# A written table for the order of TensorE's tasks and of the loads, in a kernel of windowed attention and a multiplicative feed-forward layer

## The chip, the core and the metric

The kernel runs on one core of a Trainium2 chip. The metric is the device time of one execution in microseconds, the median of several runs; the times and places in the text are microseconds, places from the start of the profiled span.

## The reference

Attention over 4 batches, 8 heads, 768 positions and head dimension 64, in which each query sees the first 4 keys (sinks) and the last 128; then a feed-forward layer that is linear but for one product.

```python
scores = scale * np.matmul(q, k.transpose(0, 1, 3, 2))
keep = is_sink | in_window              # first 4 keys, or 0 <= i - j < 128
a = softmax(np.where(keep, scores, -1e9))
x = (a @ v).transpose(0, 2, 1, 3).reshape(3072, 512)
out = ((x @ w1) * (x @ w2)) @ w3 @ w_out      # w1, w2: 512x1024; w3: 1024x1024; w_out: 1024x512
```

All inputs and the output are float32 in memory.

## The kernel before, in words

Everything is computed in bf16 with float32 sums. The loads turn float32 into bf16 on the way (they are issued by GpSimd, L108 to L141), but for the first block of w3, which SyncE loads as it is (L162). The two last matrices are folded into one on the chip, w3 @ w_out (`w3o`). TensorE's work is cut into tasks, each a generator that a planner steps through (L468 to L690); the first step is the part on TensorE, the next ones are copies and products on ScalarE and VectorE, and a last one may be a DMA on SyncE. The names of the tasks, which the text uses, are a kind and its indices:

- `t3.i.j` (`fold_w3`): eight 128x128 transposes of block i of w3 (four each for the float32 block 0: t3.0.0 and t3.0.4), and a copy out of PSUM. `fm.i.n` (`fold_mm`, L380): the fold of block i with half n of w_out: eight matmuls of 256 columns.
- `tpk.b.t`, `tpq.b.t`: transposes of k and q of batch b, 256 positions t (t is 0, 1 or 2), for batches 0 and 1; batch 0 holds positions in pairs and is transposed in pieces of 64 rows (`transposes_paired`, L228). Batches 2 and 3 are transposed by DMAs that SyncE issues (`td`, L237).
- `sc.b.r.t` (`scores`): the scores of a pair of heads r, with exponentials on ScalarE (L284) and the mask on VectorE (L288); some carry the scores of the sinks (L270). `sv.b`: the sinks' values. `av.b.r.t` (`values`): weights times values, then divided by their sum on VectorE (L314, L317).
- `xt.b.r.t`: transposes of x for batches 0 and 1 (`x_transposes`), and `xd` (L337), the same by DMA on SyncE for batches 2 and 3.
- `g.b.c.dt.h` (`gate`, L350): one of 8 column blocks dt of x @ w1 (h is 0) or x @ w2 (h is 1), four matmuls of 256 or 384 columns; h = 0 is copied by ScalarE, h = 1 multiplied by VectorE. `p.b.m` (`project`, L390): 128 rows of the output, eight matmuls of 512 columns, a copy by ScalarE and a DMA.

Four PSUM buffers (`mm`) are shared by all tasks but the scores, which have two of their own (`sc`). A task on TensorE needs its buffer free, so it waits for the copy of the fourth task back.

The planner has made-up arrival times of the loads (`arrive`, L407 to L466) and costs of each step. As it runs while the program is built, the order that comes out is fixed in the program: `pe_pick` (L586) takes at each point the task that can start first by its model, then by priority; ScalarE, VectorE and SyncE take the step that is ready first. If the model sees TensorE idle over 0.5 us before 40 us, and a PSUM buffer free, it puts in matmuls of zeros (`keep_busy`, L404; `pz` in the profile).

The order of the loads is a list (L146). After three of them come the mask tables that GpSimd makes (`affine_select`: identities, masks, sink masks); the framework may still move instructions on GpSimd, and does: it puts q and v of batch 2 ahead of most of its k. Each load is a DMA of 0.25 MB, as bf16; a half of w_out has 0.5 MB, and 0.125 MB the blocks of v and those of batches 1 to 3. In the trace GpSimd stops when eight are on their way (at 17.8 it goes on as the first half of w_out lands). k and q of batch b lie in the buffers of batch b - 2.

## Time and profile before

| | us |
|---|---|
| median of 4 runs (lowest, highest) | 202.45 (202.33, 202.77) |
| the profiled execution | 202.95 |
| its span in the profile | 201.2 |
| TensorE busy | 194.8 |
| VectorE busy | 114.5 |
| ScalarE busy | 102.6 |
| zero matmuls, recorded | 39 |

In the profile PE is TensorE's matmuls, PEld its weight loads, DVE VectorE, ACT ScalarE, POOL GpSimd and SP SyncE. A group of instructions is given by its line, engine, operation, what it writes and reads, its shape and number; then its busy time, the mean of one in ns, and the idle time before it with what ended that. A line of waits reads: who, for whom, us in total, times, longest. The chain of work that ended last follows the program back from its last instruction; a piece of it has its start, its length and what ran. The recorded length of one matmul (309 ns for a gate's) holds its latency, as they overlap; the pace is read from the chain, where eight fold matmuls take 0.87.

### The profile page before, as it was taken

What the parts mean: (1) busy time and instruction counts of PE and PEld (TensorE: products, weight loads), DVE (VectorE), ACT (ScalarE), POOL (GpSimd) and SP (SyncE); (2) the same over time, 40 slices, a digit from 0 to 9 for tenths busy, and PEclk for the clock granted to TensorE, in tenths of its full rate; (3) what the DMA queues carried; (4) which work ended last, traced back from release to release, by engine and by line L of the source; (5) the groups of instructions that cost most, each with busy time, mean ns of one, the idle gap of its engine ahead of it and who ended that gap; (6) DMA issues with size and microseconds to landing.
All of it is one profiled execution on the core that took longest, in us unless ns stands there. A gap on an engine that the chain in (4) does not pass through costs nothing.

```text
span 201.2 us, 4659 instructions
## 1 busy us (share of the span) xinstructions
PE 194.8 (97%) x1875; PEld 126.5 (63%) x1888; DVE 114.5 (57%) x267; ACT 102.6 (51%) x175; POOL 72.9 (36%) x98
## 2 busy tenths in 40 slices
PE   7999999999999999999999999999999999999992
PEld 2556987887887786566666555565666556665440
DVE  5176636695788767169777656473788404444000
ACT  2106424734866775676757466455756343333331
POOL 7991566769996998351341000000000000000000
PEclk9999999999999999999999999999999999999999
DMA  6999999999999999999999999612004251000242
GB/s 135 166 161 197 187 192 199 193 170 155 154 153 164 151 156 150 133 185 185 155 130 133 155 158 316 134 54 57 0 0 54 88 173 57 0 0 0 107 155 105
DMA packets 99158, 26.27 MB, mean 131 GB/s; under 512 B 88896, under 2 KB 95040, under 8 KB 99136
## 3 DMA queue, kind: packets, MB, share of 16 engines
q0 software_dynamic: 75952, 14.42, 90.5%
q1 hardware_dynamic: 23184, 11.54, 29.2%
q8 instruction: 15, 0.25, 0.5%
q14 instruction: 7, 0.06, 0.1%
HBM read 29.36 MB, written 6.29 MB: 177 GB/s over the span
## 4 chain that ended last, share of the span: by engine, by line
PE 96%; DVE 1%; issue 1%; ACT 0%; ACTq 0%
PE pg L350 42%; PE po L390 20%; PE av L310 7%; PE pw L380 7%; PE sc L276 6%; PE pz L404 5%; PE tp L369 2%; PE tp L228 2%; PE xt L326 1%; PE tp L214 1%; PE sp L270 1%; PE vp L251 1%; DVE qT L231 1%; DVE kT L231 1%; ACT o_sb L394 0%
## 5 line engine op out<-in xcount | busy, mean ns | idle before, releaser
L350 PE MATMUL pg<-xT,w_sb 128*128 128x384 bf16 (+1 forms) x576 | 90.1, 309 | 0.0
L350 PEld LDWEIGHTS <-w_sb 128*128 128x128 bf16 x576 | 53.7, 98 | 25.8 <-issue 1.7
L354 DVE TENSOR_TENSOR ab<-a_sb,pg 128x384 bf16<-128x384 f32 (+1 forms) x72 | 36.5, 508 | 32.1 <-PE pg L350 26.7
L284 ACT ACTIVATE ex<-sc 128x1024 bf16<-128x1024 f32 (+1 forms) x48 | 44.9, 955 | 12.9 <-PE sc L276 12.1
L357 ACT COPY a_sb<-pg 128x384 f32<-128x384 f32 (+1 forms) x72 | 31.9, 443 | 36.5 <-DVE ab L354 19.8
L390 PE MATMUL po<-w3o,ab 128*128 128x512 bf16 x180 | 43.0, 379 | 0.6
L288 DVE TENSOR_TENSOR am<-ex,maskt 128x1024 bf16<-128x1024 bf16 (+1 forms) x48 | 30.3, 641 | 6.2 <-ACT ex L284 6.2
L390 PEld LDWEIGHTS <-ab 128*128 128x128 bf16 x192 | 18.2, 98 | 20.1 <-issue 0.3
L394 ACT COPY o_sb<-po 128x512 f32<-128x512 f32 x24 | 14.0, 585 | 26.4 <-PE po L390 26.1
L317 DVE TENSOR_TENSOR xn<-av,rec 128x256 bf16<-128x256 f32 x48 | 20.4, 425 | 1.7
L111 POOL DMA_DIRECT2D vN<-in_v_dram x18 | 16.1, 903 | 10.1 <-DMA kN<-in_k_dram 5.9
L310 PE MATMUL av<-vN,am 128*128 128x65 bf16 x352 | 18.9, 193 | 0.0
L310 PEld LDWEIGHTS <-am 128*128 128x128 bf16 x352 | 16.9, 97 | 3.1 <-DVE am L288 0.2
L111 POOL DMA_DIRECT2D kN<-in_k_dram x18 | 16.1, 901 | 7.2 <-DMA kN<-in_k_dram 4.0
L111 POOL DMA_DIRECT2D qN<-in_q_dram x18 | 16.1, 895 | 6.3 <-DMA vN<-in_v_dram 3.1
L314 DVE RECIPROCAL rec<-av 128x4 f32<-128x4 f32 x48 | 8.6, 178 | 14.5 <-PE av L310 14.3
L380 PE MATMUL pw<-wo_sb,w3t 128*128 128x256 bf16 x128 | 15.8, 273 | 0.0
L276 PE MATMUL sc<-qT,kT 64*128 64x128 bf16 (+1 forms) x256 | 13.9, 238 | 0.4 <-DVE kT L231 0.4
L404 PE MATMUL pz<-ksbd 128*128 128x512 bf16 x39 | 12.4, 468 | 1.3 <-DVE ksbd L164 1.3
L380 PEld LDWEIGHTS <-w3t 128*128 128x128 bf16 x128 | 11.9, 98 | 1.5 <-issue 0.2
L310 PE MATMUL av<-vs,es 128*128 128x130 bf16 x64 | 12.3, 221 | 0.0
L276 PEld LDWEIGHTS <-kT 64*128 64x128 bf16 x256 | 8.2, 94 | 6.1 <-issue 4.4
(62 smaller groups left out, 115.1 us busy)
## 6 DMA issues: line engine op xcount, KB each, us to landing
out_dram<-o_sb SPq DMA_DIRECT2D x24, 256.0 KB, 2.3
vN<-in_v_dram POOLq DMA_DIRECT2D x24, 128.0 KB, 8.3
kN<-in_k_dram POOLq DMA_DIRECT2D x18, 128.0 KB, 7.6
qN<-in_q_dram POOLq DMA_DIRECT2D x18, 128.0 KB, 7.8
w_sb<-in_moe_w_dram POOLq DMA_DIRECT2D x8, 256.0 KB, 10.2
ab<-in_moe_w_dram POOLq DMA_DIRECT2D x7, 256.0 KB, 9.4
wo_sb<-in_moe_w_out_dram POOLq DMA_DIRECT2D x2, 512.0 KB, 9.6
qN<-in_q_dram POOLq DMA_DIRECT2D x3, 256.0 KB, 9.4
```

Of the source, the lines that this page charges most:

```text
L111: nc.gpsimd.dma_start(out=dst, in_=rows(src, b, kb))
L276: nc.tensor.matmul(sc[:, e, c:c + n], kT[b][hp, r, kb * P:(kb + 1) * P], qT[b][hp, r, qb * P:qb * P + n], start=True, stop=True)
L284: nc.scalar.activation(ex[:, :, c0:], sc[:, :, c0:], ACTF.Exp, scale=scale)
L288: nc.vector.tensor_mul(am[:, :, c0:], ex[:, :, c0:], mk)
L310: nc.tensor.matmul(o, lhs, rhs, start=(n == 0), stop=(n == len(todo) - 1), skip_group_check=True)
L317: nc.vector.tensor_mul(xns[b, t][:, :, r, :, :], av[:, :, :, 0:D], rec[:].to_broadcast([P, 2, 2, D]))
L350: nc.tensor.matmul(pg[:], w_sb[:, kk, dt * P:(dt + 1) * P], xT[b][:, kk, tk], start=(kk == 0), stop=(kk == NP - 1))
L354: nc.vector.tensor_mul(ab[b][:, dt, tk], gate_a.pop((b, c, dt))[:], pg[:])
L357: nc.scalar.copy(a_sb[:], pg[:])
L380: nc.tensor.matmul(po[:], w3T[i][:, j, :], wo_sb[:, j, n0:n1], start=(j == 0), stop=(j == KFF - 1))
L390: nc.tensor.matmul(po[:], ab[b][:, kk, m * P:(m + 1) * P], w3o[:, kk, :], start=(kk == 0), stop=(kk == KFF - 1))
L404: nc.tensor.matmul(pz[:], idle[:, 0:P], idle[:, 0:512], start=True, stop=True)
```

## The change

It has these parts.

- The planner's choice on TensorE is replaced by a table of names, `PLAN`, in which every task of TensorE stands once; `pe_pick` takes the next name and waits for it. On the other engines the planner goes on as before, with new costs. A change of tiling of TensorE's array (full, rows for scores, columns for the paired transposes) costs 0.096 in its model.
- The loads come in another order: k and q of positions 0 to 511 of batch 0 first, one half of w_out a load later than before, its second half two later, w1 and w2 behind all of w3. GpSimd is told to keep the order as written. The identities are made after the second load, the masks after the third, the sink masks after the fourth.
- Zero matmuls are counted with 0.43 us each up to 6.5 us and 0.22 after, less one, and only if three PSUM buffers are free. In the built program there are 13 instead of 40.
- The paired transposes of batch 0 are cut into halves (two pairs of heads), and their copies, those of x and those of the output go to ScalarE or VectorE, as the planner finds, instead of to a fixed one.
- In the planner's order of SyncE, a DMA transpose of batch 2 or 3 now comes at least 12 us after TensorE's transposes of batch 0 or 1 that read the same buffer (`late`).

The diff, cut:

```diff
-    order = [("q", 0, 0), ("w3", 6), ("w3", 3), ("k", 0, 0), ("v", 0, 0), ("wo", 0, 256), ("wo", 256, 512),
-             ("w1", 0, 256), ("w3", 4), ("w3", 1), ("w3", 2), ("v", 0, 1), ("k", 0, 1), ("q", 0, 1),
...
+    order = [("q", 0, 0), ("k", 0, 0), ("k", 0, 1), ("q", 0, 1), ("v", 0, 0), ("w3", 4), ("wo", 0, 256), ("w3",
+             3), ("wo", 256, 512), ("w3", 2), ("w3", 7), ("v", 0, 1), ("w3", 5), ("w3", 6), ("w3",
+             1), ("w1", 256, 512), ("w2", 256, 512), ("k", 0, 2), ("q", 0, 2), ("w1", 768, 1024),
+             ("w2", 768, 1024), ("w2", 512, 768), ("v", 0, 2), ("w2", 0, 256), ("w1", 0, 256),
+             ("w1", 512, 768)] + [
              ("qkv", b, 0, 6) for b in range(1, B)]
-    EARLY = 3
...
+    masks = {2: make_idents, 3: make_masks, 4: make_sink_masks}
+    with tc.manual_schedule(engines={mybir.EngineType.Pool}):
+        for n, x in enumerate(order):
+            if n in masks:
+                masks[n]()
+            load(*x)
...
-    def transposes_paired(src, dst, t):
+    def transposes_paired(src, dst, t, r0, me):
...
-        tp = ps_mm.tile([P, NP, 2, P], BF16, tag="mm", name="tp")
-        for r in range(NP):
+        tp = ps_mm.tile([P, 2, 2, P], BF16, tag="mm", name="tp")
+        for r in range(2):
...
-        nc.scalar.copy(xT[b][:, r0:r0 + 2, t * 256:(t + 1) * 256],
-                       xt[:].rearrange("p r i m -> p r (i m)"))
+        copy_on(me, xT[b][:, r0:r0 + 2, t * 256:(t + 1) * 256], xt[:].rearrange("p r i m -> p r (i m)"))
...
-        nc.scalar.copy(o_sb[:], po[:])
+        copy_on(("p", b, m), o_sb[:], po[:])
...
+    PLAN = """
+        t3.0.4 tpq.0.0.2 tpq.0.0.0 tpk.0.0.0 tpk.0.0.2 sc.0.0.0 t3.0.0 sc.0.1.0 tpk.0.1.0 tpq.0.1.2
+        tpq.0.1.0 tpk.0.1.2 sc.0.2.0 sv.0 av.0.0.0 av.0.1.0 sc.0.3.0 t3.4.0 sc.0.0.1 sc.0.1.1 av.0.2.0
+        xt.0.0.0 fm.4.0 av.0.3.0 t3.3.0 fm.0.0 xt.0.2.0 sc.0.2.1 sc.0.3.1 fm.3.0 fm.3.1 fm.0.1 t3.2.0
+        fm.4.1 t3.7.0 fm.2.1 fm.2.0 fm.7.1 av.0.0.1 t3.5.0 av.0.1.1 fm.7.0 av.0.2.1 fm.5.1 av.0.3.1
+        xt.0.0.1 t3.1.0 fm.5.0 t3.6.0 xt.0.2.1 fm.1.0 fm.1.1 g.0.0.2.0 g.0.1.3.0 g.0.1.3.1 tpq.0.2.0
...
+    SWITCH = 0.096
...
+        est = max([free["pe"] + (SWITCH if tiled(k) != tiling else 0.0)] + [arrive[x] + HOP for x in k["loads"]])
...
+    plan = [tuple(int(x) if x.isdigit() else x for x in name.split(".")) for name in PLAN.split()]
+
     def pe_pick():
+        if plan:
+            k = tasks[plan[0]]
+            est = earliest(k)
+            return None if est is None else (0, k, est)
         best = None
...
-                if gap > 0.5 and start < WARM_UNTIL and rings["mm"][0][0] is not None \
-                        and rings["mm"][0][0] <= max(free["pe"], START):
-                    keep_busy(int((gap - 0.25) / 0.22))
+                spins = int((max(0.0, min(start, 6.5) - max(free["pe"], START)) / 0.43
+                             + max(0.0, start - max(free["pe"], START, 6.5)) / 0.22) - 1.0)
+                if spins > 0 and gap > 0.5 and start < WARM_UNTIL and all(
+                        c[0] is not None and c[0] <= max(free["pe"], START) for c in rings["mm"][:3]):
+                    keep_busy(spins)
```

## The prediction

> **What bounds the kernel now.** I read the page first: who is busy, the chain that ended last, and what zero matmuls (`pz`, L404) cost.

> ```profile
> PE 194.8 (97%) x1875; PEld 126.5 (63%) x1888; DVE 114.5 (57%) x267; ACT 102.6 (51%) x175; POOL 72.9 (36%) x98
> ...
> PE pg L350 42%; PE po L390 20%; PE av L310 7%; PE pw L380 7%; PE sc L276 6%; PE pz L404 5%; PE tp L369 2%; PE tp L228 2%; PE xt L326 1%; PE tp L214 1%; PE sp L270 1%; PE vp L251 1%; DVE qT L231 1%; DVE kT L231 1%; ACT o_sb L394 0%
> ...
> L404 PE MATMUL pz<-ksbd 128*128 128x512 bf16 x39 | 12.4, 468 | 1.3 <-DVE ksbd L164 1.3
> ```

> TensorE is the bound almost from end to end, and 5% of the chain is multiplication by zero. The waits of TensorE say the same:

> ```profile
> PE pz L404 <- DVE ksbd L164: 1.3, 1, 1.3
> PE sc L276 <- DVE kT L231: 0.4, 1, 0.4
> PE sp L270 <- DVE qT L231: 0.3, 1, 0.3
> ```

> So the other engines matter only where they would make TensorE wait, and the time can fall in two ways: fewer zero matmuls, or fewer tiling changes. Then the chain in order of time (start, us, what):

> ```profile
> 1.33 6.90 PE pz L404 x18
> 8.23 0.87 PE tp L369 x8
> 9.10 1.29 PE pz L404 x6
> 10.40 0.57 PE tp L228 x16
> ...
> 13.26 0.59 PE tp L228 x16
> 13.87 1.24 DVE kT L231
> 15.15 0.50 PE sc L276 x8
> 15.65 0.32 PE vp L251
> 15.98 1.29 PE pz L404 x6
> 17.27 0.44 PE sc L276 x8
> ...
> 88.34 0.55 PE sc L276 x12
> 88.88 0.76 PE pg L350 x4
> ...
> 96.47 0.65 PE pg L350 x4
> ```

> The zeros at the start last until 8.23, though asked one issue at a time the trace has the raw w3 block landed at 4.20 and q at 6.85 (its transposes start at 10.40). The granted clock in the trace is full only from 7.12 on: till then zeros are 0.43 apart, later 0.215. From 18 on there are no zeros, and TensorE is full. Last pair above: a gate of four matmuls takes 0.65, and 0.76 right behind scores.

> **The change, part by part.**

> *Zeros.* The order of the built kernels has 40 before (39 recorded) and 13 after (6, then half of t3.0, then 7). On the chain the old ones take 5.3% of 201.2 = 10.7. New: 6 x 0.43 = 2.6, from 1.33 to 3.9; t3.0.4 waits for the block (4.20) and for the fp32 identity, which is behind q and k at GpSimd (about 4.0); its 4 transposes take 0.44 warm, so about 0.87 cold, to 5.1; the 7 zeros run at 0.43 up to 7.12 and then at 0.215, to about 7.6. That is 5.1 of zeros: 5.6 less. This is a gain only where real work fills the place, so I place the work.

> *First attention.* q (6.85) is transposed at 7.6 instead of 10.4. k is now second at GpSimd: 1.3 behind q (two 0.25 MB loads behind q land 1.33 and 1.29 apart), 8.2. Copies are halved (about 0.69 on VectorE, 0.6 on ScalarE, from the 128x512 rows of L207 and L330, instead of 1.23 for one at L231) and lie on both engines. VectorE has the four copies of ones_s ahead of them, and these wait for the sink masks, now behind two more loads at GpSimd: about 8.1, so VectorE's first copy ends near 9.3. The first scores start about 9.4 instead of 15.15. Behind them come t=1's k and q (about 9.8 and 11.2), v (13.2), t3.4 (14.7) and the first two scores of t=1: some 6 us of work between 8 and 17, all waiting for loads.

> *The load that decides: the first half of w_out (wo0).* Fold matmuls (L380), the work that fills TensorE from 18 on in both, need it. Before, 1.25 MB (as bf16) are ahead of it and it landed at 17.52; its other half, 0.5 MB more, at 20.16. After, 1.5 MB are ahead of it (k and q of t=1 come first, two w3 blocks later), so it ends at 2.0 MB: halfway, 18.8. The other bound is 17.0: the last v (13.16), 1.3 for a w3 block and 2.6 for wo0 itself. I take 18.3, nearer to the landings. The rest follows at 1.3 per 0.25 MB; all loads up to v of t=2 have the same sum (46.35 before), so what comes behind keeps its times. GpSimd, which issues them, is now in a fixed order; k of batch 2, landed at 71.87 before because q and v were put ahead, comes sooner.

> *From wo0 on.* From fm.4.0 to fm.1.1 the table holds 14 folds x 0.873 = 12.2, six w3 transposes x 0.445 = 2.7, av 0.18 + 4 x 0.357 = 1.6, xt 3 x 0.22 = 0.7, one pair of scores 0.65: 17.9. From 18.4, with 0.35 for w3 block 3 (19.7), it ends at 36.6. The other loads are there at least 0.6 ahead of use by the same steps.

> Now compare with before at 35.93, where TensorE has 161.6 to go (to 197.5, its last matmul). Relative to that point, after at 36.6 has done two folds more (1.75), two scores of t=1 (0.66), four av (1.43), two xt (0.45), and four gate halves less (1.75): 2.5 less to go, 0.7 later. Lead: **1.9**. So of 5.6 us of zeros two thirds come back as waits ahead of wo0.

> *Tiling changes.* The two orders have 65 changes of tiling before, 60 after. By the rows above a change costs about 0.1: the gate behind scores takes 0.76, not 0.65. [...] By the row: 0.5, most of it ahead of 36.6, where waits hide it; behind that point I count 0.1. [...]

> *New waits later.* The table is rigid: TensorE waits for the next name, while everything behind it in PE's queue waits too. Places where it nears a transfer: tpq.1.2 needs q of batch 1's last block, landed at 63.14 before. From 36.6 the table has 25.6 of work and some 12 changes, so it gets there at 63.4: just in time. With wo0 at 17.0 TensorE would be there at 62.1 and lose 1 again, so the lead has a ceiling near 2.3 unless loads land sooner. g.2.0.5.0 needs xd.2.1, which follows av.2.3.1 by 8.2 us before (114.2 to 122.5); the table puts 9.1 of work between, but SyncE has transposes of batch 3 queued ahead, so 0 to 1. The sinks of batch 2 need its last q transpose: the table reaches them about 3 sooner than before (103.41), and the out-DMAs and transposes ahead on SyncE are sooner too: 0 in my sum, 1 as bound. xt, o_sb and transpose copies may now go to either engine; at 57% and 51% busy I cost this at nothing while four PSUM buffers cover it; a missed buffer costs 0.2 to 0.4 each time. I put 0.3 for all of these together.

> *The end.* One ScalarE copy (0.58), then the DMA (about 2): unchanged. Five projections last instead of seven, no price.

> Sum: -1.9 - 0.1 + 0.3 = **-1.7**. The profiled execution took 202.95 (span 201.2, 1.75 around it): 201.25, span 199.5. The median is 0.50 below the profiled run, so 202.45 - 1.7 = **200.75**.

> **The rivals.**

> *The clock falls back (slower).* The zeros between 8.9 and 17.3 also kept TensorE busy; now it works perhaps 60% of 8 to 18. The trace shows the clock rising 5.8 us after the first matmul, and never an idle stretch before the end, so it can't tell when it falls. [...] If sparse work and transposes count as idle, the folds at 18.3 begin at half clock; with 5.8 us to recover, half of that is lost, 2.9: 200.75 + 2.9 = 203.6 (an estimate from the trace's own 5.8). With 3.4 us cold the whole lead is gone; from there it is slower. Chance 0.16.

> *The table stalls.* Late loads or full PSUM buffers eat the lead: wo0 at 18.8 (-0.5), 1 at xd.2.1, some small ones: about 202.1. For: a fixed order can't step around a late load, and landings jump (58.98, then 61.41, two loads in a row before). Against: most of its work has a margin. Chance 0.16, about 0.06 faster, 0.07 the same, 0.03 slower.

> *Loads land sooner.* wo0 near 17 and batch 1 half a us ahead, since GpSimd issues big loads closer together at the start (4.64 and 5.89 before for the third and fourth): -2.9, 199.55. Chance 0.13.

> *The zeros were free* (hidden loads, no gain) is in the second: the folds would have to start over 2 us later.

> **How the numbers follow.** The likeliest, chance 0.55, is 200.75; its own range is 200.1 to 201.7. A measurement of this kernel tells 0.2% (0.4 us) from no change. Faster by more: 0.55 + 0.13 + 0.06 = 0.74; same 0.07 + 0.02 (a small clock loss) = 0.09; slower 0.03 + 0.14 = 0.17. The range 199.3 to 202.6 takes in the likeliest, most of the sooner loads and the stalls, some 0.8; it leaves out the clock rival's upper part.

> **What would show it.** Right: 13 zeros; q transposes near 7.6, first scores near 9.4, first fold near 18.4; TensorE waiting 3 to 5 us in all between 8 and 19 and less than 1 behind; fm.1.1 done near 36.6; the clock full from about 7 on. Wrong: a second half-clock stretch, folds of 1.7 behind 18; a first fold later than 19.5; waits of TensorE on q, xT or PSUM readers that sum to over 2 behind 36.

## The result, and the profile after

The changed kernel takes 201.56 (median of 40 runs, 200.31 to 203.44), the kernel before, timed again beside it, 202.79 (59 runs, 202.02 to 204.07): a ratio of 0.9936 (95% interval 0.9922 to 0.9949). That is 1.2 us less where 1.7 was forecast. The profiled execution took 201.96, its span is 200.3.

The page of the changed kernel, cut: busy times, the busy share of TensorE (PE) and its granted clock in 40 slices of 5.0, and the chain.

```profile
PE 191.7 (96%) x1848; PEld 126.1 (63%) x1861; DVE 115.9 (58%) x274; ACT 102.2 (51%) x174; POOL 73.0 (36%) x98
...
PE   7969999999999999999999999999999999999992
...
PEclk9985999999999999999999999999999999999999
...
PE pg L352 42%; PE po L392 20%; PE av L312 7%; PE pw L382 7%; PE sc L278 6%; DMA ab<-in_moe_w_dram 3%; PE tp L371 2%; PE xt L329 1%; PE tp L216 1%; POOL qN L134 1%; POOL kN L134 1%; PE sp L272 1%; POOL vN L137 1%; PE tp L230 1%; PE vp L253 0%
```

Three things are to be seen. The zeros have gone from the chain. In their place the chain has loads and GpSimd, which issues them: the start is now bound by loads openly. And the granted clock has a dip, 8 and 5 tenths in the third and fourth slices (10 to 20), where before it was full:

```profile
PEclk9999999999999999999999999999999999999999
```

TensorE in order of time (start, us, what, idle before it):

```profile
5.10 2.63 PE L406 MATMUL pz<-ksbd 128*128 128x512 bf16 x7
7.66 0.64 PE L230 MATMUL tp<-ident,qN 128*64 128x128 bf16 x16
...
9.37 0.34 PE L278 MATMUL sc<-qT,kT 64*128 64x256 bf16 x4 [0.46 <-ACT kT L209]
...
13.98 0.58 PE L253 MATMUL vp<-vN,sel 128*128 128x512 bf16 x1 [1.72 <-DMA vN<-in_v_dram]
...
19.02 1.85 PE L382 MATMUL pw<-wo_sb,w3t 128*128 128x256 bf16 x8
...
21.34 1.04 PE L382 MATMUL pw<-wo_sb,w3t 128*128 128x256 bf16 x8
```

Up to the scores this is the prediction's timetable. But the first fold takes 1.85 recorded (1.04 later on; 1.64 and 0.87 on the chain), and starts 0.4 behind its load (18.61): the chain comes from w3 block 4, which landed at 15.97, through 3 us of work at half clock. TensorE in five stretches, cut every 3.41 from the first change of the granted clock (the stretch, its length, busy time and number of matmuls, granted clock, share of DMA, GB/s):

```profile
3.61:7.03 3.42, 3.26 (x11) 1.00 1.43 137
7.03:10.44 3.41, 2.95 (x47) 1.00 1.73 167
10.44:13.85 3.41, 1.60 (x40) 1.00 1.66 156
13.85:17.27 3.42, 3.03 (x29) 0.50 1.32 181
17.27:20.68 3.41, 3.41 (x34) 0.50 1.36 199
```

One thing about such rows: the record of the clock begins with its first rise (7.03 here, 7.12 in the kernel before), and a row ahead of that prints 1.00, though zeros are 0.43 apart there. Up to the first rise only the pace of the work tells the clock.

The clock fell to half at 13.85, right behind a stretch of 3.41 in which TensorE was busy for 1.60, and came back at 20.68. That is the prediction's first rival, come true in part, and one of its signs of being wrong. It doesn't happen in each execution. Two of the 40 runs (203.41 and 203.44), over 1.5% above the fastest, count as slow and are left out of this comparison. Of the other 38, 19 have a mean clock of 0.995 or more and a median of 201.1; 11 lie between 0.985 and 0.995, with 201.54; 8 are below, with 202.4. A half-clock stretch of 3.41 takes 0.0085 off the mean (half of 3.41 in 200.3), so by this estimate these are runs with none, about one and about two. The 57 runs of the kernel before whose clock was read beside the experiments are all at 0.996 or more. So in the runs at full clock the change brings 202.79 - 201.1 = 1.7, and the dip goes with some of it lost in half of the runs; the next experiment fills the gap to see whether it is the cause.

### The profile page after: what moved, and what is told of

Its sections match the earlier page's. It is cut to its first block, busy times and chain, and to the rows that moved or that the text cites. A ratio compares the mean times of both kernels' runs of the same rounds, so it can differ in the third digit from the quotient of the medians.

```text
span 200.3 us, 4595 instructions
## 1 busy us (share of the span) xinstructions
PE 191.7 (96%) x1848; PEld 126.1 (63%) x1861; DVE 115.9 (58%) x274; ACT 102.2 (51%) x174; POOL 73.0 (36%) x98
## 4 chain that ended last, share of the span: by engine, by line
PE 90%; POOL 4%; DMA 3%; issue 1%; ACT 0%; POOLq 0%; ACTq 0%
PE pg L352 42%; PE po L392 20%; PE av L312 7%; PE pw L382 7%; PE sc L278 6%; DMA ab<-in_moe_w_dram 3%; PE tp L371 2%; PE xt L329 1%; PE tp L216 1%; POOL qN L134 1%; POOL kN L134 1%; PE sp L272 1%; POOL vN L137 1%; PE tp L230 1%; PE vp L253 0%
## 5 line engine op out<-in xcount | busy, mean ns | idle before, releaser
L352 PE MATMUL pg<-xT,w_sb 128*128 128x384 bf16 (+1 forms) x576 | 92.1, 308 | 0.0
L286 ACT ACTIVATE ex<-sc 128x1024 bf16<-128x1024 f32 (+1 forms) x48 | 44.3, 958 | 7.9 <-PE sc L278 7.4
L392 PE MATMUL po<-w3o,ab 128*128 128x512 bf16 x179 | 43.5, 379 | 0.6
L392 PEld LDWEIGHTS <-ab 128*128 128x128 bf16 x192 | 18.4, 98 | 19.9 <-issue 0.3
L290 DVE TENSOR_TENSOR am<-ex,maskt 128x1024 bf16<-128x1024 bf16 (+1 forms) x48 | 29.7, 640 | 0.7 <-ACT ex L286 0.7
L209 ACT COPY o_sb<-po 128x512 f32<-128x512 f32 x17 | 10.0, 586 | 30.3 <-PE po L392 29.0
L312 PE MATMUL av<-vN,am 128*128 128x65 bf16 x352 | 20.0, 196 | 0.0
L312 PEld LDWEIGHTS <-am 128*128 128x128 bf16 x352 | 17.3, 99 | 2.8 <-issue 0.7
L111 POOL DMA_DIRECT2D qN<-in_q_dram x18 | 16.1, 896 | 5.0 <-DMA vN<-in_v_dram 3.7
L382 PE MATMUL pw<-wo_sb,w3t 128*128 128x256 bf16 x128 | 16.6, 281 | 0.0
L209 DVE COPY o_sb<-po 128x512 f32<-128x512 f32 x7 | 4.8, 692 | 19.1 <-PE po L392 19.1
L278 PE MATMUL sc<-qT,kT 64*128 64x128 bf16 (+1 forms) x256 | 14.8, 245 | 0.5 <-ACT kT L209 0.5
L382 PEld LDWEIGHTS <-w3t 128*128 128x128 bf16 x128 | 12.4, 101 | 1.8 <-issue 0.2
```

The source lines that it names most:

```text
L111: nc.gpsimd.dma_start(out=dst, in_=rows(src, b, kb))
L209: (nc.scalar.copy if home[me] == "act" else nc.vector.tensor_copy)(dst, src)
L278: nc.tensor.matmul(sc[:, e, c:c + n], kT[b][hp, r, kb * P:(kb + 1) * P], qT[b][hp, r, qb * P:qb * P + n], start=True, stop=True)
L286: nc.scalar.activation(ex[:, :, c0:], sc[:, :, c0:], ACTF.Exp, scale=scale)
L290: nc.vector.tensor_mul(am[:, :, c0:], ex[:, :, c0:], mk)
L312: nc.tensor.matmul(o, lhs, rhs, start=(n == 0), stop=(n == len(todo) - 1), skip_group_check=True)
```

## The experiments

Nine kernels, one of them timed twice on different chips, each against the kernel before on its chip. To compare them I use two marks of each trace: the start of the first fold, and the end of `fm.1.1`, which is the 14th fold in the tables. For the kernels that share the table from there on, what is late there is late at the end (the last table below).

### Filling the gaps

Zero matmuls are put ahead of three tasks that wait for loads.

```diff
+    EXTRA = {("sv", 0): 7, ("t3", 4, 0): 4, ("fm", 4, 0): 3}
...
+                if k["name"] in EXTRA:
+                    keep_busy(EXTRA[k["name"]])
+                    rings["mm"] = rings["mm"][1:] + [[max(free["pe"], START)]]
```

> The changed kernel with 14 zero matmuls more, in three gaps in which TensorE waits for loads: 7 ahead of sv.0, 4 ahead of t3.4.0, 3 ahead of fm.4.0. Theory (the granted clock fell to half from 13.9 to 20.7 since the stretch from 10.4 to 13.9 was too empty; folds at half pace cost about 1.3): the clock stays full, the first fold starts near 18.7 and takes 0.87, fm.1.1 is done near 36.6 instead of 37.8, and the time is about 1.0 below the changed kernel's median, near 200.5, with less spread from run to run. Rival (the missing 0.4 to 1.3 are stalls on loads or PSUM further on, the clock costs nothing since loads set the pace until 22): the same time as the changed kernel, or up to 0.5 slower for the zeros.

> The filled kernel again, for the comparison with the others on one chip: within 0.3 of the filled kernel's first time (0.992 of the kernel before) and at full clock in every run.

Measured: 201.28 and 201.36, ratios 0.9923 (0.990 to 0.9945) and 0.9915 (0.9889 to 0.9942); all twelve runs are at 0.996 or more, and lie between 200.69 and 201.71. The first folds of the second one, from its chain (18.49 and 20.25), where the changed kernel's chain has 1.64 and 0.87:

```profile
18.49 0.92 PE pw L382 x8
...
20.25 0.87 PE pw L382 x8
```

The first fold starts at 18.37, and fm.1.1 ends at 36.59 (36.91 in the first) instead of 37.84. So the clock theory holds: filled, no run dips, and the folds take 0.92 and 0.87. The size falls short of the 1.0 expected, since half of the changed kernel's runs hardly dip anyway: medians differ by 0.2 to 0.3, and the intervals of the two ratios overlap, so that the gain of filling in the median is not shown. Against the 8 runs with the longest dip (202.4) it is 1.1. This is the steadiest version of the study.

### The old order with fewer zeros

```diff
-                    keep_busy(int((gap - 0.25) / 0.22))
+                    keep_busy(int((gap - 0.25) / 0.22) if start < 6.0 else 1)
```

> The kernel before, its 18 first zeros kept, the 22 zeros of the six later groups cut to one each. Theory (zeros there hold the clock up; loads set the pace until wo0): TensorE waits in their place, the clock falls in some runs, and the time is 0 to 1.5 above the kernel before. Rival (each zero on the chain costs its 0.215): 16 x 0.215 = 3.4 faster.

Measured: 204.23, ratio 1.0052 (1.0022 to 1.0083): 0.5% slower. Its waits (who, for whom; us in total):

```profile
PE pw L380 <- DMA wo_sb<-in_moe_w_out_dram: 1.6, 1, 1.6
...
PE tp L228 <- DMA kN<-in_k_dram: 1.1, 1, 1.1
PE sc L276 <- DVE kT L231: 1.0, 1, 1.0
PE sc L276 <- ACT ex L284: 0.8, 2, 0.4
```

The zeros that went came back as waits, 4.8 in all where the kernel before has 0.7; the largest is for wo0. The three runs at full clock took 202.28, 202.72 and 203.07, which is the kernel before's time (202.78 beside it); the other nine, with mean clocks of 0.98 to 0.99, 203.6 to 205.1. So the middle zeros were worth nothing as time on the chain and 1.5 to 2 as a hold on the clock.

### A late start, and no zeros at all

For the late start, zeros are put ahead of the first transposes by the same added lines as above.

```diff
+    EXTRA = {("tpq", 0, 0, 2): 13}
```

> The changed kernel with 13 zeros more ahead of the first transposes of q, so that real work starts near 10.4 as in the kernel before. Theory (the first half of w_out sets when the folds start, not the first transposes): the first fold still starts within 0.6 of 18.7; the denser work up to then may keep the clock up, so the time is 0.5 slower to 1.0 faster than the changed kernel. Rival (the gain is the earlier start itself): 2.5 slower than the changed kernel, slower than before too.

Measured: 201.34, ratio 0.9932 (0.9908 to 0.9955). Eleven of its twelve runs are at full clock, so the fair comparison is the filled kernel on the same chip: 201.28. The transposes of q start at 10.33 instead of 7.66 in the changed kernel, the first fold at 18.57, and fm.1.1 ends at 36.93 (36.91 in the filled kernel). An earlier start by 2.7 is worth nothing.

```diff
-                if spins > 0 and gap > 0.5 and start < WARM_UNTIL and all(
+                if False and gap > 0.5 and start < WARM_UNTIL and all(
```

> The changed kernel without any zero matmul. Theory (zeros only keep the clock; loads set the pace): real work starts at the same landings (q near 6.8), but the clock rises late, only after the folds have begun, so 2 to 3 slower than the changed kernel, and slower than the kernel before: 203.5. Rival (13 zeros in place of 40 is where the gain is): faster than the changed kernel by up to 0.8, as q is transposed sooner.

Measured: 201.56, ratio 0.9942 (0.9918 to 0.9965), the changed kernel's, and 0.2 above the filled kernel on the same chip (201.36), within the noise. Both sides of my expectation are wrong. The clock rises at 15.18 here. Up to then work runs at half pace (16 transposes take 1.06, where the change has 0.64), but in time:

```profile
8.81 1.06 PE L230 MATMUL tp<-ident,kN 128*64 128x128 bf16 x16 [1.31 <-DMA kN<-in_k_dram]
...
14.32 0.61 PE L253 MATMUL vp<-vN,sel 128*128 128x512 bf16 x1
...
18.42 1.03 PE L382 MATMUL pw<-wo_sb,w3t 128*128 128x256 bf16 x8 [0.18 <-DMA wo_sb<-in_moe_w_out_dram]
```

Loads leave so much room ahead of 18 that TensorE can do its part at half clock. The zeros at the start buy nothing that can be told from noise in this kernel; what matters is that the clock is up when the folds begin.

### The new loads without the table, in two ways

For the first the table of the changed kernel is emptied: the planner picks, and the new loads, costs and split copies stay. The second is the kernel before with nothing but the new list of loads.

> The changed kernel with an empty table, so that the planner picks TensorE's next task by its model; the new order of loads, split copies and new costs stay; 7 zeros are left. Theory (table and loads order matter through what is done ahead of w_out): the greedy order does about the same ahead of wo0, so between the changed kernel and the kernel before, 201 to 203, and it is open to the clock as well. Rival (the table itself is the gain): as slow as before or slower, 203 or more.

> The kernel before with the changed kernel's list of loads and nothing else of the change: no table, the old costs and zeros (33 of them), the old copies. Its planner then does much the same ahead of wo0 as the table (k and q of t=1 and two scores of it). Theory (the order of loads makes the gain, the table only fits TensorE's order to it): most of the gain, 0.8 to 1.8 below the kernel before, near 201.5. Rival (the table is the gain): no faster than the kernel before.

Measured: 205.85 (ratio 1.0145, 1.0116 to 1.0175) and 206.29 (1.0188, 1.0156 to 1.0221): both slower than before, and both against my theory. The waits of TensorE in the second one, whose mean clock in the trace is 1.0, cut:

```profile
PE pw L380 <- DMA wo_sb<-in_moe_w_out_dram: 1.3, 1, 1.3
PE po L390 <- ACT o_sb L394: 1.1, 1, 1.1
PE sc L276 <- DVE qT L231: 0.8, 1, 0.8
PE sc L276 <- ACT ex L284: 0.5, 1, 0.5
```

With the others it waits 4.6, aside from 1.3 ahead of the first zeros, where the kernel before waits 0.7; its 33 zeros are 7 fewer (1.5). Its last matmul ends at 200.86, 3.4 later than before (197.49), so about 1 of that is not accounted for. Half of the waits lie ahead of its first fold (19.34, with wo0 landed at 19.30), and 1.1 at 120. Emptied, the changed kernel waits more still, 5.8, 1.4 of it at 64; its first fold starts at 20.44, and its clock was at half from 10.5 to 20.7 in the trace. So the new loads with a planner that picks by its model make no gain, with the old costs or the new. The opposite, a table with the old loads, was not run; the split copies and the `late` rule were not tried by themselves either.

### Splitting the pairs of scores

In 17 places of the table, for example:

```diff
-        av.1.0.0 sc.1.2.0 sc.1.3.0 g.0.2.5.0
+        av.1.0.0 sc.1.2.0 g.0.2.5.0 sc.1.3.0
```

> The changed kernel with the three gaps filled (as in e1_fill_gaps), and in batches 1 to 3 the second of two neighbouring scores moved behind the task that follows it, 17 times: the same work, 34 changes of tiling more (94 for 60). Theory (a change costs about 0.1 on TensorE, nothing hides it behind 36): 34 x 0.1 = 3.4 slower than the filled kernel, 204.7. Rival (the array changes tiling for next to nothing, and what one sees behind a pair is only its last matmul's tail): within 0.5 of it, up to 1 slower for exponentials that come later.

The filled kernel is the base here. Measured: 206.0, 4.6 above it on the same chip (201.36). One place on the chain of the filled kernel, then the same of the split one:

```profile
101.25 0.55 PE sc L278 x12
101.80 1.41 PE pg L352 x8
```

```profile
104.16 0.33 PE sc L278 x6
104.49 0.76 PE pg L352 x4
105.24 0.33 PE sc L278 x6
```

Two scores together take 0.55, apart 0.66, and each gate behind one takes 0.76 instead of 0.65: 0.22 for two changes more. In the traces TensorE's last matmul ends 4.57 later; 1.25 of it is one stall at 82.6 (values that wait for a mask on VectorE), and fm.1.1 was 0.2 earlier. No other gap of TensorE over 0.15 can be seen behind 36 in the two traces. So 34 changes cost 4.57 - 1.25 + 0.2 = 3.5, 0.10 each. The price of the prediction holds.

### Where w_out stands among the loads

First, wo0 one place sooner, with the fold of block 0 first:

```diff
-    order = [("q", 0, 0), ("k", 0, 0), ("k", 0, 1), ("q", 0, 1), ("v", 0, 0), ("w3", 4), ("wo", 0, 256), ("w3",
+    order = [("q", 0, 0), ("k", 0, 0), ("k", 0, 1), ("q", 0, 1), ("v", 0, 0), ("wo", 0, 256), ("w3", 4), ("w3",
```

> The changed kernel with the first half of w_out loaded one place earlier (before w3 block 4), the fold of block 0 put first in the table, block 4 behind it, and the gaps ahead of sv.0 and of the first fold filled with 7 and 3 zeros. Theory (wo0's landing sets the pace): wo0 lands near 17.3, the first fold starts there instead of 18.7, and as the second half of w_out is needed next and comes no sooner, some 0.4 to 0.9 of it is kept: 0.5 below the filled kernel. Rival (another load, or q of batch 1, sets the pace behind it): no difference from the filled kernel.

Measured: 202.83, ratio 1.0013 (0.9993 to 1.0033): the gain is lost, 1.5 above the filled kernel beside it. wo0 landed at 18.16, hardly sooner (18.32 in the filled kernel beside it), and my few changed names made waits of their own: 1.1 for a copy of w3 block 4 on ScalarE, 0.9 for a mask, 0.8 for the sink keys. fm.1.1 ended at 38.66.

Then wo0 third, and w_out ahead of v and of t=1's k and q, with the head of the table rewritten to follow:

```diff
+    order = [("q", 0, 0), ("k", 0, 0), ("wo", 0, 256), ("w3", 4), ("wo", 256, 512), ("w3", 3), ("v", 0, 0),
+             ("w3", 2), ("k", 0, 1), ("q", 0, 1), ("w3", 7), ("v", 0, 1), ("w3", 5), ("w3", 6), ("w3", 1),
```

> The changed kernel with w_out ahead of v, and of k and q of positions 256 to 511 (loads: q, k, wo0, w3 block 4, wo1, w3 block 3, v, w3 block 2, k, q, then as in the changed kernel), and the first 53 names of the table put in an order that follows these loads; the rest of the table as it is; 11 zeros more. Theory (the loads set TensorE's pace up to about 20, and a load is worth what work it sets free: w_out and a w3 block more than k, q and v): wo0 lands near 12.4, TensorE is full from about 15 on, fm.1.1 ends near 35.3 instead of 36.6, and the time is 1.3 below the filled kernel (e1_fill_gaps), about 200.0, unless q of batch 1 (61.3) stops it. Rival (wo0 is late by its own, 8 to 9 behind its issue, wherever it stands; the pace is set further on): within 0.3 of the filled kernel, or slower.

Measured: 204.82, ratio 1.0117 (1.0089 to 1.0145). TensorE of this kernel:

```profile
12.36 1.03 PE L382 MATMUL pw<-wo_sb,w3t 128*128 128x256 bf16 x8
...
19.48 0.38 PE L253 MATMUL vp<-vN,sel 128*128 128x512 bf16 x1 [1.00 <-DMA vN<-in_v_dram]
...
38.67 1.92 PE L382 MATMUL pw<-wo_sb,w3t 128*128 128x256 bf16 x16 [0.56 <-DVE w3t L209]
```

The load did as forecast (12.22) and the fold follows it at once. TensorE was not full from 15 on, though: it waited for v, for VectorE's divisions that now come in a bunch, for masks (1.0) and for copies, 3.3 in gaps that can be seen and 0.9 in zeros that the planner put in, and fm.1.1 ended at 40.59. Whether a table searched for this order of loads would win was not tried.

### What comes behind is the same for all

The end of fm.1.1 and of TensorE's last recorded matmul, in the traces of the kernels that share the table from there on:

| kernel | first fold | fm.1.1 ends | TensorE ends | between |
|---|---|---|---|---|
| filled gaps, second | 18.37 | 36.59 | 195.50 | 158.9 |
| filled gaps, first | 18.71 | 36.91 | 195.75 | 158.8 |
| late start | 18.57 | 36.93 | 195.59 | 158.7 |
| no zeros | 18.42 | 37.38 | 196.04 | 158.7 |
| the change | 19.02 | 37.84 | 196.50 | 158.7 |
| wo0 sooner | 18.29 | 38.66 | 197.33 | 158.7 |
| w_out first | 12.36 | 40.59 | 199.25 | 158.7 |

Within 0.3 the rest of the table takes 158.7 whatever went before: TensorE is the bound there with nothing else in its way. What sets these seven kernels apart is decided in the first 41 us.

## Why the prediction was right

The direction and the mechanism were right, the size was 1.7 for a measured 1.2. In the profiled run TensorE's last matmul ends 1.0 earlier than before (196.50 for 197.49): fm.1.1 is 1.2 later than forecast, and what follows it takes 158.7 instead of 159.3 (161.6 - 2.5 - 0.1 + 0.3), 0.6 less.

- *Zeros and first attention.* Right to a tenth: q's transposes at 7.66 (7.6), scores at 9.37 (9.4). But two experiments show that none of these times mattered, as the prediction's step on wo0 implies and didn't say: start 2.7 later, or at half clock without zeros, and the time is the same within noise.
- *wo0.* Taken at 18.3, landed at 18.61 (18.32 and 18.16 elsewhere). The value was right, in part by luck: the last v and w3 block 4 ahead of it landed at 14.69 and 15.97, not at 13.2 and 14.7. The reasoning by bytes ahead of it is doubtful: moved one load forward it gained 0.2 to 0.5 instead of 1.3. In the kernel before, the changed, the second filled, the "wo0 sooner" and the "w_out first" kernels it landed 8.7, 8.5, 8.2, 8.6 and 8.4 behind its issue; but in the two kernels of the new loads without the table, 9.1 and 9.3. What sets it is not settled.
- *The lead at fm.1.1.* Forecast 36.6; in the filled kernel, at full clock, 36.59 and 36.91; in the changed kernel's profiled execution 37.84. This is the term that was off, and its cause is shown: folds and what stands ahead of them at half clock, 0.9 to 1.25 between the traces, and gone when the gaps are filled. The prediction had it as a rival with 2.9 and a chance of 0.16. It should have been a share of the likeliest case: a dip that comes in half of the executions and costs up to 1.3.
- *When the clock falls.* The prediction had no trace in which it falls while there is work, and left open when it would. In the change's trace the longest gap of TensorE was 1.72 (ahead of v), and the stretch of 3.41 ahead of the fall held 1.81 idle; with the empty table it held two gaps of 0.89 and 0.83. The rival had sparse work and transposes count as idle: the fall came behind sparse work, and no run shows that transposes count as idle (the last section).
- *Tiling.* 0.1 each, measured 0.10 by itself. Little of the five changes fewer can reach the end, as said.
- *Waits later.* I put 0.3; there were none. No gap of TensorE over 0.12 can be seen behind 16.1 in the changed kernel's trace, and 158.7 repeats. q of batch 1 landed at 61.60, 1.5 sooner than before and well ahead of TensorE, which came for it at 64.47; the ceiling of 2.3 was not reached.
- *The rivals.* Stalls of the table: not in this one, but in both tables whose head I rewrote by hand and in both kernels that let the planner pick. Loads sooner: wo0 not, batch 1 yes, but nothing waited for it. "The zeros were free" was right about the zeros, and no rival to the gain, which comes from what is done by the time w_out is there: from the start of the first fold to its last matmul TensorE takes 179.7 in the kernel before (17.83 to 197.49) and 177.1 in the second filled one (18.37 to 195.50).

## What to carry to other kernels

Zeros on the critical chain aren't a gain that waits to be taken: look for the load that comes next on TensorE's path, and count only what is done ahead of it. Where the filler was taken out here, TensorE was busy 1.60 of a stretch of 3.41, and the clock was at half for the 6.83 behind it: when filler goes, reckon with that, and fill that gap alone. Choose an order of loads together with an order of tasks: the new loads without the table were slower than the kernel before, and in two other orders of loads, with a table fitted to them by hand, the gain was lost.

## What the runs showed of the hardware

The stretches below are of the kernels "old order with fewer zeros" (two), "empty table" (one) and "no zeros" (two):

```profile
10.82:14.24 3.42, 1.79 (x26) 1.00 1.70 164
14.24:17.65 3.41, 1.17 (x16) 1.00 1.33 175
...
7.09:10.50 3.41, 1.70 (x44) 1.00 1.69 162
...
8.35:11.77 3.42, 2.71 (x26) 1.00 1.80 152
11.77:15.18 3.41, 3.41 (x50) 1.00 1.42 160
```
